# A retention block and two MLPs on one core: another bank for two products at the head, a conversion started one unit later, and a new order of a seven-product pair

## The chip, the cores and the metric

The program runs on one core of one Trainium2 chip. A core has five engines that run side by side and wait for each other through semaphores: PE (TensorE, matrix products), DVE (VectorE), ACT (ScalarE), POOL (GpSimd) and SP (SyncE, which here only issues transfers). Every engine works through its own list of instructions in order. Results of PE go to banks of PSUM, a small memory of eight banks; ACT and DVE read them from there. The metric is the time of one execution on the device in microseconds (us), the median of several runs.

## The reference, cut to what matters

```python
# retention: 2 batches, 8 heads, 768 positions, 64 wide, blocks of 64
intra = (qb @ kb.T * Dmask) @ vb
inter = (qb * lam_pow) @ kv_state
out[block] = intra + inter
kv_state = lam_block * kv_state + (kb * rev_pow).T @ vb
...
x = out as 1536 tokens x 512
h = max(x @ w_in, 0);  x = (h * h) @ w_out        # first MLP, 2048 hidden
h = x @ w_in2;         y = max(0.01 * h, h) @ w_out2   # second MLP
```

The four weight matrices are float64, everything else is float32.

## The kernel before

**Retention** (function `retention`) takes the two batches in 12 units of 128 positions. For each unit, PE transposes k and q (`transposes`, L287 to L300; PE rows with L294), ACT copies the two banks to `kT` and `qT` (L298), PE makes the products of q and k (`scores`, L311), DVE multiplies them with the decay table `DTr` (`mask`, `Pm`, L316), DVE scales q for the carried state (`scale_q`, `qS`, L304), PE makes the new state's product (`state`, L335; it takes `kd`, a decayed k of POOL) and the output (`output`, L360 and L362). ACT and DVE then split the output into a high and a low part, `xhi` and `xlo` (`split`, L68 and L69). The order of PE and SP is that of the code (a manual schedule); the order of ACT, DVE and POOL is set by the scheduler. `bank()` hands out the next PSUM bank in turn, and the instruction that writes it first has to wait until the bank's last reader is through. A bank named `idle` takes transposes without use at the very start.

**Conversion of weights.** A megabyte of float64 words (a tile `raw`) is loaded by SP, and `converting` turns it to float32 step by step: an absolute value on ACT (L114, tile `hb`), six steps on DVE (L115, L116, L118, L121, L122, L125), then a cast of the high part on ACT (L135) and the low part on DVE (L137). `convert()` takes one step at each call. In retention it is called once a unit, for the units 3 to 9, with the step pinned to its place in the order.

**MLPs.** A layer takes the hidden 2048 in four slices s, and the 1536 tokens in three tiles of 512. A float32 product is made of three reduced ones: high by high, high by low, low by high (`three`, L503). `first` makes the hidden values of a tile, one bank m of 128 at a time, in 12 products; ACT and DVE make high and low parts of the activation from it: tiles `g0h`, `g0l` of token tile 0 and `g1h`, `g1l` of token tile 1 (index m, 0 to 3). `second` multiplies by the second weights.

For layer 0, slices 1 and 2 (`seven`), the second products of token tiles 0 and 1 are made with seven block products in place of eight (`second_pair`). The blocks of the weights are A11, A12, A22 and the sums S1 to S4; those of the tokens are B11, B21, B22 and the sums T1 to T4 (`four_sums`, DVE L449 to L451; its results are split by a cast on ACT, L68, and a subtraction on DVE, L69). Each of them is done for p = 0 and p = 1, six matrix products each, on a bank per p. Two block products can share a bank: S4 by B22 goes on adding to the bank C of S1 by T1, after this has been copied. `keep` copies a bank with ACT (L609) to a buffer f, and sends it to a tensor in memory: by SP where it is the first value, by POOL with an addition in memory where it is not (L613). The tensors `partial` hold P1 (A11 by B11), P6 and P67; after the last slice of `seven`, ten additions from memory to memory, issued by POOL (L684), combine them.

Of the kernel before, what the change touches and what calls it, by code (L numbers as in the profile page):

```python
# [19 lines left out]
def tile_retention_then_two_mlps(  # L20
# [163 lines left out]
    def retention(ctx_att, att):  # L184
# [9 lines left out]
        nats, qT, kT, qS, Pm, raw_scores = {}, {}, {}, {}, {}, {}  # L194
# [82 lines left out]
        def column_of_powers():  # L277
            ps = bank()[:, 0:H]
            nc.tensor.transpose(ps, pw[:, 1:C + 1], ident[0:H, 0:H])
            nc.scalar.copy(kdec, ps)  # L280
# [7 lines left out]
        def transposes(i, names="kq"):  # L288
            for name in names:
                dst = {"k": kT, "q": qT}[name]  # L290
                ps = bank().rearrange("p (a s) -> p a s", a=NP)
# [31 lines left out]
        def state(n):  # L323
# [8 lines left out]
            ps = bank()[:, 0:NP * D].rearrange("p (a e) -> p a e", a=NP)  # L332
# [51 lines left out]
        state(0)  # L384
        mask(0)
        output(0)
        scale_q(2, transposes(2))
# [3 lines left out]
        for i in range(n_units):  # L391
# [16 lines left out]
            if 3 <= i <= 9:  # L408
                convert(pin=True)
# [195 lines left out]
    partial = [{n: dram.tile([P, TT], F32, name=f"partial{p}{n}") for n in ("P1", "P6", "P67")} for p in range(2)]  # L605
# [11 lines left out]
    def second_pair(s):  # L617
        begun = (0, s - 1) in seven
# [35 lines left out]
        for p in both:  # L654
            keep(product(p, "A", "A11", "B11"), partial[p]["P1"], not begun)
            yield True
        for p in both:
            keep(product(p, "C", "S1", "T1"), kept(p, 1, 1), False)
            yield True
        late_split("T3", "T1", lambda h: (1, 2 * h))  # L660
        for p in both:
            keep(product(p, "A", "A12", "B21", False), kept(p, 0, 0), False)
            yield True
        late_split("T4", "B21", lambda h: (0, 2 * h + 1))
        for p in both:
            keep(product(p, "C", "S4", "B22", False), kept(p, 0, 1), False)
            yield True
        for p in both:
            keep(product(p, "B", "S2", "T2"), partial[p]["P6"], not begun)
            yield True  # L670
# [4 lines left out]
        for p in both:  # L675
            keep(product(p, "B", "S3", "T3", False), partial[p]["P67"], not begun)
            yield True
        opened.add(("sums", 0, s + 1))
        if (0, s + 1) not in seven:
            for p in both:  # L680
                p1, p6, p67 = (partial[p][n] for n in ("P1", "P6", "P67"))
                for dst, src in ((p67, p1), (kept(p, 0, 1), p1), (kept(p, 0, 1), p6), (kept(p, 1, 0), p67),
                                 (kept(p, 1, 1), p67)):
                    nc.gpsimd.dma_start(dst, src, accum_op=ALU.add, max_dma_last_dim=TT)  # L684
# [46 lines left out]
    def stage(l, s):  # L731
# [4 lines left out]
        if l == 0:  # L736
            parts = [first(l, s, t, ms) for ms in (range(2), range(2, 4)) for t in range(2)]
        else:
# [43 lines left out]
```

## Time and profile before

| | |
|---|---|
| runs | 576.01, 576.70 and 577.94 us, median 576.7 |
| profiled execution | 576.42 us, its span 574.5 us |
| PE busy | 564.2 us of the span, 98% |
| DVE, ACT, POOL busy | 418.4, 305.0 and 83.9 us |
| granted TensorE clock | 1.000 over the span |

The span goes from the first instruction to the last; 1.92 us of the profiled execution lie outside of it. Busy time is the time in which an engine had an instruction at work, and the rest is waiting. Products of PE follow each other before the one ahead has ended: a product of 512 columns is listed with 0.39 us, and the next begins after 0.23.

### The profile page before, as it was taken

Reading aid. Unit: us, or ns where it says so; the run is one execution under the profiler, and the core shown is the slowest. Engines: PE = TensorE matmul, PEld = TensorE weight load, DVE = VectorE, ACT = ScalarE, POOL = GpSimd, SP = SyncE. Lnnn points to the kernel's source line nnn. Section 1 sums busy time; section 2 is a strip of 40 time slices with the busy share of each in tenths; the row PEclk is TensorE's granted clock in tenths of the full one; section 3 lists DMA queues with packets and bytes.
Section 4 is the critical chain, followed back from the end, with each engine's and each line's share of the span. In section 5 each row is a group of like instructions: output and inputs, shape, how many; then the busy total and the mean of one; then the engine's idle time right before and its main releaser. Section 6 shows DMA issues by size and latency. Waiting matters only on the chain.

```text
span 574.5 us, 8051 instructions
## 1 busy us (share of the span) xinstructions
PE 564.2 (98%) x3075; PEld 470.7 (82%) x3075; DVE 418.4 (73%) x589; ACT 305.0 (53%) x477; POOL 83.9 (15%) x101
## 2 busy tenths in 40 slices
PE   7989999999999999999999999999999999999997
PEld 6878888888788888888888888888888888888886
DVE  3879999999927599498478999929873996217222
ACT  2344598546757687758448374553562376225110
POOL 3426000000040105445000000000203011310000
PEclk9999999999999999999999999999999999999999
DMA  8997434665492649999713216341529523661432
GB/s 172 239 213 177 156 121 138 234 183 180 172 164 57 73 148 181 203 249 189 185 36 91 76 41 216 128 165 74 103 55 246 109 29 47 76 90 56 162 113 92
DMA packets 74071, 78.12 MB, mean 136 GB/s; under 512 B 40105, under 2 KB 46513, under 8 KB 74033
## 3 DMA queue, kind: packets, MB, share of 16 engines
q1 hardware_dynamic: 60448, 60.57, 34.6%
q0 software_dynamic: 13056, 16.78, 20.9%
q8 instruction: 24, 0.39, 0.3%
q10 hardware_dynamic: 528, 0.26, 0.2%
q14 instruction: 15, 0.11, 0.1%
HBM read 52.43 MB, written 27.80 MB: 140 GB/s over the span
## 4 chain that ended last, share of the span: by engine, by line
PE 74%; DVE 15%; DMA 6%; issue 3%; SPq 1%; ACT 1%; POOL 0%; DVEq 0%; POOLq 0%; ACTq 0%
PE ps L503 72%; DMA raw<-in_moe_w_in 2%; DVE rb L122 2%; DMA raw<-in_moe_w_out 2%; DVE hb L125 2%; DVE hb L118 2%; SPq L65 1%; DVE rb L121 1%; DVE hb L115 1%; DVE Pm L316 1%; DMA k<-in_k 1%; DVE xlo L69 1%; DVE w1l L137 0%; DVE g1l L474 0%; DVE sw L442 0%
## 5 line engine op out<-in xcount | busy, mean ns | idle before, releaser
L503 PE MATMUL ps<-xhi,w1h 128*128 128x512 f32 x288 | 112.1, 389 | 0.0
L503 PE MATMUL ps<-xlo,w1h 128*128 128x512 f32 x288 | 112.0, 389 | 0.0
L503 PE MATMUL ps<-xhi,w1l 128*128 128x512 f32 x288 | 112.0, 389 | 0.0
L613 POOL DMA_DIRECT2D spill<-f x48 | 46.9, 1047 | 347.6 <-ACT f L609 347.5
L609 ACT COPY f<-ps 128x512 f32<-128x512 f32 x84 | 48.9, 586 | 74.1 <-PE ps L503 72.7
L503 PEld LDWEIGHTS ps<-xhi,w1h 128*128 128x128 f32 x288 | 54.1, 188 | 11.3 <-issue 0.2
L503 PEld LDWEIGHTS ps<-xlo,w1h 128*128 128x128 f32 x288 | 54.1, 188 | 11.3
L503 PEld LDWEIGHTS ps<-xhi,w1l 128*128 128x128 f32 x288 | 54.1, 188 | 11.2
L474 DVE TENSOR_TENSOR g0l<-f,g0h 128x512 fp32r<-128x512 f32 x52 | 35.1, 687 | 33.7 <-ACT f L470 22.1
L503 PE MATMUL ps<-w2l,g0h 128*128 128x512 f32 (+1 forms) x132 | 50.5, 383 | 0.0
L503 PE MATMUL ps<-w2h,g0l 128*128 128x512 f32 (+1 forms) x132 | 50.5, 383 | 0.0
L503 PE MATMUL ps<-w2h,g0h 128*128 128x512 f32 (+1 forms) x132 | 50.5, 383 | 0.0
L137 DVE TENSOR_TENSOR w2l<-hb,w2h 128x1024 fp32r<-128x1024 f32 x16 | 19.5, 1222 | 39.8 <-ACT w2h L135 39.8
L114 ACT ACTIVATE hb<-raw 128x1024 f32<-128x1024 f32 x32 | 36.8, 1150 | 19.2 <-DVE w2l L137 7.4
L503 PE MATMUL ps<-g0h,w2h 128*128 128x512 f32 x104 | 40.5, 389 | 0.0
L503 PE MATMUL ps<-g0l,w2h 128*128 128x512 f32 x104 | 40.5, 389 | 0.0
L503 PE MATMUL ps<-g0h,w2l 128*128 128x512 f32 x104 | 40.5, 389 | 0.0
L122 DVE SCALAR_TENSOR_TENSOR rb<-raw,rb 128x1024 f32<-128x1024 uint32 x32 | 39.1, 1221 | 0.4
L125 DVE TENSOR_TENSOR hb<-hb,rb 128x1024 f32<-128x1024 f32 x32 | 39.1, 1220 | 0.4
L118 DVE SCALAR_TENSOR_TENSOR hb<-raw,hb 128x1024 uint32<-128x1024 uint32 x32 | 39.1, 1220 | 0.3
L567 DVE TENSOR_TENSOR f<-ps,f 128x512 f32<-128x512 f32 x40 | 26.2, 684 | 9.9 <-PE ps L503 9.9
L714 DVE TENSOR_TENSOR f<-ps,f 128x512 f32<-128x512 f32 (+1 forms) x25 | 16.7, 669 | 22.9 <-PE ps L503 21.7
(141 smaller groups left out, 1139.4 us busy)
## 6 DMA issues: line engine op xcount, KB each, us to landing
raw<-in_moe_w_in SPq DMA_DIRECT2D x16, 1024.0 KB, 5.6
raw<-in_moe_w_out SPq DMA_DIRECT2D x16, 1024.0 KB, 5.0
spill<-f POOLq DMA_DIRECT2D x48, 256.0 KB, 4.8
spill<-f SPq DMA_DIRECT2D x24, 256.0 KB, 2.6
f<-spill SPq DMA_DIRECT2D x24, 256.0 KB, 2.9
k<-in_k SPq DMA_DIRECT2D x12, 256.0 KB, 4.9
q<-in_q SPq DMA_DIRECT2D x12, 256.0 KB, 5.1
v<-in_v SPq DMA_DIRECT2D x12, 256.0 KB, 4.8
```

The lines of the kernel that those rows point to most:

```text
L65: return nc.sync.dma_start(dst, src)
L114: nc.scalar.activation(hf, w_hi.bitcast(F32), AF.Abs)
L118: yield ve.scalar_tensor_tensor(out=hb, in0=w_hi, scalar=0xC0000000, in1=hb, op0=ALU.bitwise_and, op1=ALU.bitwise_or)
L122: yield ve.scalar_tensor_tensor(out=rf, in0=w_lo, scalar=2.0 ** -52, in1=rf, op0=ALU.mult, op1=ALU.mult)
L125: yield ve.tensor_tensor(out=hf, in0=hf, in1=rf, op=ALU.add)
L137: yield ve.tensor_tensor(out=lo, in0=hf, in1=hi, op=ALU.subtract)
L474: nc.vector.tensor_tensor(out=glo, in0=r, in1=ghi, op=ALU.subtract)
L503: nc.tensor.matmul(ps, a, b, start=start and n == 0, stop=stop and n == len(ops) - 1, skip_group_check=again)
L567: ve.tensor_tensor(out=out, in0=ps[h, where], in1=other, op=ALU.add)
L609: nc.scalar.copy(f, src)
L613: nc.gpsimd.dma_start(dst, f, accum_op=ALU.add)
L714: nc.vector.tensor_tensor(out=a, in0=ps, in1=a, op=ALU.add)
```

## The change

Three things change. At the head of retention, the small transpose of `column_of_powers` writes to the bank `idle`, the transposes of unit 2's k take the bank of unit 1's q, the product of `state(0)` takes the bank of unit 1's k, and the transposes of unit 2's k are written ahead of `mask(0)` and `output(0)`. The pinned steps of conversion are made in the units 4 to 10. In `second_pair`, A11 by B11 comes ahead of the first layer's last bank (m = 3 of token tile 1, which moves into the pair), A12 by B21 comes ahead of S1 by T1, and S4 by B22 follows S1 by T1 directly; each slice has `partial` tensors of its own, and makes its own ten additions.

```diff
         def column_of_powers():
-            ps = bank()[:, 0:H]
+            ps = idle[:, P:P + H]
...
-                ps = bank().rearrange("p (a s) -> p a s", a=NP)
+                whole = bank() if (i, name) != (2, "k") else read[1, "q"]
+                read[i, name] = whole
+                ps = whole.rearrange("p (a s) -> p a s", a=NP)
...
-            ps = bank()[:, 0:NP * D].rearrange("p (a e) -> p a e", a=NP)
+            whole = bank() if n else read[1, "k"]
+            ps = whole[:, 0:NP * D].rearrange("p (a e) -> p a e", a=NP)
...
         state(0)
+        transposes(2, "k")
         mask(0)
         output(0)
-        scale_q(2, transposes(2))
+        scale_q(2, transposes(2, "q"))
         state(1)
...
-            if 3 <= i <= 9:
+            if 4 <= i <= 10:
                 convert(pin=True)
...
-    partial = [{n: dram.tile([P, TT], F32, name=f"partial{p}{n}") for n in ("P1", "P6", "P67")} for p in range(2)]
+    partials = {
+        s: [{n: dram.tile([P, TT], F32, name=f"partial{s}{p}{n}") for n in ("P1", "P6", "P67")} for p in range(2)]
+        for _, s in seven
+    }
...
         for p in both:
-            keep(product(p, "A", "A11", "B11"), partial[p]["P1"], not begun)
-            yield True
+            keep(product(p, "A", "A11", "B11"), partial[p]["P1"], True)
+            yield True
+        yield from first(0, s, 1, (3,))
+        for p in both:
+            keep(product(p, "A", "A12", "B21", False), kept(p, 0, 0), False)
+            yield True
+        late_split("T4", "B21", lambda h: (0, 2 * h + 1))
         for p in both:
             keep(product(p, "C", "S1", "T1"), kept(p, 1, 1), False)
             yield True
         late_split("T3", "T1", lambda h: (1, 2 * h))
         for p in both:
-            keep(product(p, "A", "A12", "B21", False), kept(p, 0, 0), False)
-            yield True
-        late_split("T4", "B21", lambda h: (0, 2 * h + 1))
+            keep(product(p, "C", "S4", "B22", False), kept(p, 0, 1), False)
+            yield True
         for p in both:
-            keep(product(p, "C", "S4", "B22", False), kept(p, 0, 1), False)
-            yield True
-        for p in both:
-            keep(product(p, "B", "S2", "T2"), partial[p]["P6"], not begun)
+            keep(product(p, "B", "S2", "T2"), partial[p]["P6"], True)
             yield True
...
-        if (0, s + 1) not in seven:
-            for p in both:
-                p1, p6, p67 = (partial[p][n] for n in ("P1", "P6", "P67"))
+        for p in both:
+            p1, p6, p67 = (partial[p][n] for n in ("P1", "P6", "P67"))
...
+            if (l, s) in seven:
+                parts[-1] = first(l, s, 1, (2,))
```

On PE at the head, this stands in the order of before, from `scores(1)` (L311) on; L335 is `state(0)`, then L362 `output(0)`, then the transposes (L294) of unit 2:

```order
L311 MATMUL ps<-qT,kT 128x128 x7
L335 MATMUL ps<-v,kd 64x64 [waits DMAHW6_49,DVE_49,Pool_49]
L335 MATMUL ps<-v,kd 64x64 x7
L362 MATMUL ps<-Pm,v 64x128 [waits PE_49]
L362 MATMUL ps<-Pm,v 64x128 [waits DVE_49]
L362 MATMUL ps<-Pm,v 64x128 x6
L294 MATMUL ps<-ident,k 128x128 [waits DMAHW0_49]
```

and this in that of the change, where the same instructions are L313, L338, L365 and L296:

```order
L338 MATMUL ps<-v,kd 64x64 [waits DMAHW6_49,Pool_49]
L338 MATMUL ps<-v,kd 64x64 x7
L296 MATMUL ps<-ident,k 128x128 [waits DMAHW0_49,DVE_49]
L296 MATMUL ps<-ident,k 128x128 x3
L365 MATMUL ps<-Pm,v 64x128 [waits PE_49]
L365 MATMUL ps<-Pm,v 64x128 x7
```

`state(0)` has lost its wait for DVE, and unit 2's k transposes have moved ahead of `output(0)` and gained one (for `scale_q(1)`, the last reader of their new bank).

On ACT, the piece around the first absolute value of the conversion (L114) reads in the change as follows; xhi_282 are the casts of the outputs 0 to 2, kT and qT those of the units 2 to 4:

```order
L300 COPY kT<-ps 128x512
L68 CAST xhi_282<-ps 128x4x128
L300 COPY qT<-ps 128x512
L300 COPY kT<-ps 128x512
L300 COPY qT<-ps 128x512
L68 CAST xhi_282<-ps 128x4x128
L300 COPY kT<-ps 128x512
L300 COPY qT<-ps 128x512
L68 CAST xhi_282<-ps 128x4x128
L114 ACTIVATE hb<-raw 128x1024
```

Before, the first two rows stood the other way round, and the others in the same places; L114 is the eighteenth instruction of ACT in both, and the copies for unit 5 stand behind it in both.

On ACT in the pair of slice 1, before (with the numbers of the tiles: ps_1771 and ps_1782 are the banks C of p = 0 and p = 1, ps_1749 the bank of A11 and A12 for p = 0; casts to g1h are those of T3, casts to g0h those of T4, the cast to t4 that of T2):

```order
L609 COPY f_1778<-ps_1771 128x512 [waits PE_49]
L68 CAST t4_1648<-f_1738 128x512 [waits DVE_49]
L68 CAST g1h_1598<-f_1617 128x512 [waits PE_49]
L68 CAST g1h_1598<-f_1711 128x512 [waits PE_49]
L609 COPY f_1789<-ps_1782 128x512
L609 COPY f_1805<-ps_1749 128x512 [waits DMAHW2_49,PE_49,Activation_49]
```

and in the change, where C is ps_1800 and ps_1814, and A11 and A12 lie on ps_1724 and ps_1738:

```order
L616 COPY f_1780<-ps_1724 128x512 [waits PE_49]
L68 CAST g0h_1554<-f_1592 128x512 [waits PE_49]
L616 COPY f_1790<-ps_1738 128x512 [waits DMAHW1_49,PE_49]
L616 COPY f_1807<-ps_1800 128x512 [waits DMAHW2_49,PE_49]
L68 CAST t4_1651<-f_1763 128x512 [waits DVE_49]
L68 CAST g0h_1554<-f_1692 128x512 [waits DVE_49]
L68 CAST g1h_1601<-f_1620 128x512 [waits PE_49]
L68 CAST g1h_1601<-f_1714 128x512 [waits PE_49]
L616 COPY f_1821<-ps_1814 128x512 [waits Activation_49]
```

Between the copies of the two banks C stand four casts in the change, and three before. In slice 2 the change has three casts between them (two of T3, one of T2).

## Rows read from the trace of the kernel before

**Rows 1.** The page: the span, busy time by engine, and the chain that ended last.

```profile
span 574.5 us, 8051 instructions
PE 564.2 (98%) x3075; PEld 470.7 (82%) x3075; DVE 418.4 (73%) x589; ACT 305.0 (53%) x477; POOL 83.9 (15%) x101
...
PE 74%; DVE 15%; DMA 6%; issue 3%; SPq 1%; ACT 1%; POOL 0%; DVEq 0%; POOLq 0%; ACTq 0%
```

**Rows 2.** Waits of PE: us in total, times, longest us.

```profile
PE ps L335 <- issue: 2.5, 1, 2.5
PE ps L311 <- ACT qT L298: 2.2, 3, 1.8
```

**Rows 3.** Timeline of PE at the head: start, us, instruction [idle before, releaser].

```profile
14.06 0.69 PE L335 MATMUL ps<-v,kd 128*64 128x64 f32 x16 [2.52 <-issue]
...
32.73 1.16 PE L311 MATMUL ps<-qT,kT 64*128 64x128 f32 x16 [1.76 <-ACT qT L298]
```

**Rows 4.** Timeline of DVE in retention, same columns.

```profile
13.27 1.29 DVE L316 TENSOR_TENSOR Pm<-ps,DTr 128x512 f32<-128x512 f32 x2 [6.79 <-DMA DTr<-tab]
...
31.75 1.37 DVE L115 TENSOR_SCALAR hb<-hb 128x1024 f32<-128x1024 f32 x1 [2.71 <-ACT hb L114]
...
56.71 1.22 DVE L137 TENSOR_TENSOR w1l<-hb,w1h 128x1024 fp32r<-128x1024 f32 x1
```

**Rows 5.** Timeline of ACT at the head, around the first absolute value.

```profile
30.60 1.12 ACT L114 ACTIVATE hb<-raw 128x1024 f32<-128x1024 f32 x1 [3.47 <-DMA raw<-in_moe_w_in]
...
32.09 0.59 ACT L298 COPY qT<-ps 128x512 f32<-128x512 f32 x1
```

**Rows 6.** Timeline of SP's queue: the issue of the first weights.

```profile
22.76 1.13 SPq L65 DMA_DIRECT2D raw<-in_moe_w_in  x1
```

**Rows 7.** Windows: us, busy us of each engine (x), clock, DMA share, GB/s.

```profile
64.00:155.00 91.00, 90.91 (x401) 74.95 (x400) 88.74 (x113) 64.06 (x95) 0.00 (x0) 1.00 0.48 160
...
157.00:200.00 43.00, 43.00 (x191) 35.60 (x190) 22.28 (x29) 28.46 (x45) 10.57 (x12) 1.00 0.61 103
200.00:228.00 28.00, 28.00 (x125) 23.19 (x124) 27.90 (x39) 21.91 (x37) 7.40 (x8) 1.00 0.63 156
228.00:280.00 52.00, 52.00 (x231) 43.06 (x230) 35.24 (x45) 35.78 (x54) 20.54 (x21) 1.00 1.08 201
```

**Rows 8.** Timeline of PE in the pair of slice 1: firsts of block products, and the wait.

```profile
151.12 0.39 PE L503 MATMUL ps<-g0h,w2h 128*128 128x512 f32 x1
...
153.84 0.39 PE L503 MATMUL ps<-g1h,sw 128*128 128x512 f32 x1
...
155.44 0.50 PE L503 MATMUL ps<-g1l,sw 128*128 128x512 f32 x1 [0.53 <-DVE g1l L69]
...
157.40 0.39 PE L503 MATMUL ps<-g0h,w2h 128*128 128x512 f32 x1
...
160.12 0.39 PE L503 MATMUL ps<-g1h,sw 128*128 128x512 f32 x1
```

**Rows 9.** Timeline of ACT in the pair of slice 1.

```profile
157.59 0.62 ACT L68 CAST t<-f 128x512 fp32r<-128x512 f32 x1 [0.79 <-DVE f L450]
158.12 1.14 ACT L68 CAST g1h<-f 128x512 fp32r<-128x512 f32 x2
159.16 1.06 ACT L609 COPY f<-ps 128x512 f32<-128x512 f32 x2
```

**Rows 10.** Timeline of DVE before and in the pair of slice 1.

```profile
147.35 0.69 DVE L450 TENSOR_TENSOR f<-f 128x512 f32<-128x512 f32 x1
...
154.70 0.69 DVE L69 TENSOR_TENSOR g1l<-f,g1h 128x512 fp32r<-128x512 f32 x1
```

**Rows 11.** Timeline of ACT in the pair of slice 2: the copy of bank C.

```profile
218.80 0.59 ACT L609 COPY f<-ps 128x512 f32<-128x512 f32 x1 [0.61 <-PE ps L503]
```

**Rows 12.** Timeline of DVE in the pair of slice 2.

```profile
216.54 1.22 DVE L125 TENSOR_TENSOR hb<-hb,rb 128x1024 f32<-128x1024 f32 x1
```

**Rows 13.** Waits of POOL: the longest ahead of an addition in memory.

```profile
POOL spill L684 <- DMA spill<-f: 5.8, 1, 5.8
```

## What the change does to the time: the prediction

> **What bounds the kernel now.** The page comes first: PE is busy 98% of the span, and three quarters of the chain that ended last are PE's own [rows 1]. The granted clock is 1.00 in the windows from 64 to 280 us [rows 7], so a product costs the same there. What can be won without removing products is PE's idle time, 574.5 − 564.2 = 10.3 us. The list of PE's waits names the ones that this change is about: 2.5 us ahead of `state(0)` and 1.8 us ahead of one of the `scores` [rows 2]. The timeline puts them at 14.06 and 32.73 us [rows 3], and a third of 0.53 at 155.44, in the pair of slice 1 [rows 8]. The reader is to see next what ends each of them, because a wait that is removed only pays if no later one is anchored to something that has not moved.
>
> **The head.** The wait before 14.06 is put down to "issue", but DVE's first `Pm` starts at 13.27 after 6.79 us of waiting for the decay table [rows 4]; `state(0)` was to write the bank that this `Pm` reads. In the order of the change its wait for DVE is gone. `state(0)` and what hangs on it can then start up to 2.5 us earlier. `output(0)` needs `Pm` and cannot, and the k transposes of unit 2 now wait for `scale_q(1)`, which is behind that `Pm` on DVE.
>
> What is late next is the wait at 32.73. ACT waits 3.47 us for the first weights, makes the absolute value from 30.60 on, and only then copies kT and qT of unit 5, the latter at 32.09 [rows 5]; PE's `scores` start when it is through, 32.09 + 0.59 = 32.68. The weights are issued at 22.76 in SP's row of loads [rows 6]. In the order of the change that issue and the absolute value stand where they did, ahead of the same copies. So whatever PE gains before 32.73 it waits there: 1.76 us become up to 1.76 + 2.52 = 4.28, and **the head is worth 0**. The bounds are 0 and, if the load landed so much earlier, −4.3 (the two waits together).
>
> **The conversion.** The step on DVE that filled part of the stall at 31.75 (L115, 1.37 us) [rows 4] moves behind `Pm` of unit 5, and every later step by one unit. The same steps are made, so their sum is unchanged; but DVE has lost one step's place in a stretch in which it waits, and makes it in one in which it is full: 88.74 of 91 us from 64 to 155 [rows 7]. It enters that stretch later by about that step, 0.7 to 1.4 us. The low part of the first weights was made at 56.71 [rows 4]; a unit takes about 4.5 us (12 units by 64), so it moves to 61.2 and, with the lag, to at most some 63, and the MLP's first products are at 64. This costs PE nothing, with about 1 us of cover left. If that cover were gone, PE would wait for it one for one.
>
> **The pair of slice 1.** Twelve products, one block for both p, take 153.84 − 151.12 = 2.72 us [rows 8]. S1 by T1 took 157.40 − 153.84 = 3.56, so the wait that is listed with 0.53 costs 0.84 from start to start. It ended when DVE had made the low part of T1 (154.70 + 0.69) [rows 10]. In the new order A11 runs from 148.40, m = 3 from 151.12, A12 by B21 from 153.84, S1 by T1 from 156.56, S4 by B22 from 159.28. The second half of T1 is now wanted at about 157.5; even with DVE 1.4 us later it is there at 156.8. **This gives −0.84.** A11's low part of bank 2 is wanted at 149.3; DVE makes it straight behind the row at 147.35 [rows 10], so it is ready about 148.7, and 1 us of delay there would show as a short wait.
>
> The new order brings a new wait. S4 by B22 goes on in the bank C of S1 by T1, and must wait for ACT's copy of it. Before, A12 by B21 lay between: from 157.40, when S1 by T1 had ended, to 160.12 [rows 8]. ACT had three casts to make first, from 157.59 on, and its copy of p = 1 began at 159.16 [rows 9] and took about 0.57 of the 1.06 for two: done at 159.73, which is 2.33 us after the block's end, inside the 2.72. Now only the six products for p = 0 lie between, 1.36 us. With the same lateness PE waits 2.33 − 1.36 = 0.97. Four casts stand there now in place of three (0.53 more), but the casts may begin at another time: the first hangs on a sum of DVE (L454, which was L450) over the bank m = 3. Step by step: m = 3 ends at 153.84, three activations of ACT end at about 155.9, DVE's three steps of 0.69 or less ahead of that sum and the sum itself (with up to 1 us of lag) end at 158.5 to 159.5, and four casts of 0.53 and the copy end at 161.3 to 162.4, against 160.64 when PE would begin p = 1. That is a wait of 0.7 to 1.8. It cannot be under 0.37: the casts of T3 overwrite what p = 1 reads, so two of them (1.06) and the copy (0.57) come after 159.28 whatever DVE does, with 0.1 for the signals. **I take +1.0**, the measured lateness, bounds 0.4 and 1.9.
>
> The Trainium skill bears on this in "PSUM — Partial Sum Buffer", "Engine vs sequencer instructions": the queues of ScalarE and VectorE are strictly first in, first out. By that rule the copy cannot overtake casts that wait for DVE, and the sum would be that of this paragraph; ACT's rows in the pair [rows 9] agree, the copy following the casts though its bank was full 1.76 us before.
>
> **The pair of slice 2.** The copy of C for p = 0 began at 218.80, when PE had filled it [rows 11]. In the new order the same block comes 2.72 later, so p = 1 ends at 218.75 + 1.36 + 2.72 = 222.8 and S4 by B22 wants its bank at 224.2. DVE, at 216.54 in L125 [rows 12], has eight instructions ahead of the end of L454; by the rows' durations (two of 1.22, seven of 0.69, starts a little closer) that ends at 223.1 to 223.8. Then the T2 cast and the copy, 1.1 together: 224.2 to 225.0. The least is 0.37 as above. **+0.5**, bounds 0.4 and 1.0.
>
> **Transfers.** Ten additions in memory are made once more, and six sums of slice 2 become plain stores. POOL's queue then works from about 165 to 200, where PE has no idle time and the DMA share is 0.61 [rows 7]; before, this work fell into the stretch from 228 on, at 1.08, where PE lost nothing either. By counts of 2.72 S3 by T3 ends at 181 (two blocks after 162.0, four banks of token tile 2, one block); two dependent additions with a wait of up to 5.8 us each [rows 13] and the stores of token tile 2 then leave POOL by about 200, and land by about 206. The buffers f that these free are wanted for m = 2 and the pair of slice 2, from about 212 on. I cost it at 0; if it makes the first weights of the next slice late, DVE, full from 200 to 228 (27.90 of 28) [rows 7], has no slack to give.
>
> The skill's "DMA: Bandwidth & Descriptors", "Issuing engines are not separate DMA queues", speaks against this part: transfers of all issuers run on the same 16 engines and interleave, so POOL's additions would take their share from SP's loads. No row of before shows the two together at that place. What it would do is the fourth rival below.
>
> **Sum.** 576.42 − 0.84 + 1.0 + 0.5 + 0 = 577.1 us on the profiled execution, which lies 0.3 below the median of 576.7. By the bounds: 576.42 − 0.84 + 0.8 = 576.4 to 576.42 − 0.84 + 2.9 + 0.5 (a wait at A11) = 579.0. I predict 577.2. A difference of 0.3% (1.7 us, 575.0 to 578.4) is about what a measurement of this kernel can tell from no change.
>
> **The rivals.**
> - *The head pays* (chance 0.22). The first weights land earlier since less stands ahead of them, or ACT's copies are not held; then 2.5 to 4.3 us go, and the waits of the pairs come on top: 577.1 − 2.5 = 574.6, at the best 572.8. For it speaks that the wait of 2.5 is surely released; against it that the 32.73 start hangs on the landing alone [rows 3, 5, 6].
> - *The copy is in time* (0.15): DVE is early and the waits are at their least, 576.4, or none, 575.6. The data dependence of T3's casts speaks against none.
> - *DVE is late* (0.17): its lag of 1.4 meets a full stretch [rows 7], and PE also waits at 64 us or at A11 and for T2, by 1 to 2 us: 578.5 to 579.5, slower. It decides when the lag passes the 1 us of cover.
> - *Additions hold up loads* (0.06): the combination from 165 to 200 delays the weights of slice 2 or the buffers f by more than the 6 us they have, each us beyond lost: 579 to 582.
> - The forecast itself has 0.40, its own range 576.4 to 579.0.
>
> **How the numbers follow.** Leaving out the best of the first rival and the fourth gives 574.2 to 579.6. Faster by over 0.3%: the most of the first rival and a bit of the second, 0.22. Slower: the third and fourth, and the forecast's upper end, 0.25. Within: 0.53.
>
> **What would show it.** In the changed profile the wait before `state(0)` is gone, and the one before `scores` near 32.7 is over 3 us, ended by ACT's qT; no wait for `g1l` in the first pair, but one for ACT's copy in each pair, about 1.0 and 0.5 us. Wrong would be a start of those `scores` before 31.5, a first-pair wait over 2 us or none, or a wait of PE between 33 and 148 us.

## The result, and the profile after

The changed kernel takes 583.51 us (median of 5 runs, 583.02 to 584.7), the kernel before beside it 576.43 (575.83 to 577.94): a ratio of 1.0123 (95% interval 1.0108 to 1.0138), so slower by 7.1 us. The profiled execution of the changed kernel took 584.70 us, 1.2 above its median. The forecast was 577.2 in a range from 574.2 to 579.6; it was wrong, on the slow side.

The page of the changed kernel, its span, busy time and the chain that ended last (against [rows 1]):

```profile
span 582.8 us, 8049 instructions
PE 567.8 (97%) x3075; PEld 472.3 (81%) x3075; DVE 418.7 (72%) x589; ACT 304.6 (52%) x477; POOL 87.7 (15%) x105
...
PE 70%; DVE 15%; DMA 7%; ACT 4%; issue 3%; SPq 1%; DVEq 0%; ACTq 0%
```

The span grew by 8.3 us. PE's idle time went from 10.3 to 15.0 (+4.7), and its busy time by 3.6 although it makes the same 3075 products; at least in part these ran at a lower clock. PE's waits, against [rows 2]:

```profile
PE ps L507 <- ACT f L616: 3.7, 2, 2.4
PE ps L296 <- DVE qS L306: 2.2, 1, 2.2
PE ps L313 <- ACT qT L300: 1.7, 2, 1.5
PE ps L507 <- DVE g0l L492: 1.6, 1, 1.6
```

The timeline of PE in the changed kernel says where, against [rows 3, 8] (start, us, instruction, idle before and releaser):

```profile
12.03 0.69 PE L338 MATMUL ps<-v,kd 128*64 128x64 f32 x16
14.87 0.66 PE L296 MATMUL ps<-ident,k 128*128 128x128 f32 x4 [2.15 <-DVE qS L306]
...
32.76 1.16 PE L313 MATMUL ps<-qT,kT 64*128 64x128 f32 x16 [1.47 <-ACT qT L300]
...
65.06 0.50 PE L507 MATMUL ps<-xhi,w1h 128*128 128x512 f32 x1
...
149.53 0.39 PE L507 MATMUL ps<-g0h,w2h 128*128 128x512 f32 x1
...
152.18 0.50 PE L507 MATMUL ps<-g0l,w2h 128*128 128x512 f32 x1 [1.58 <-DVE g0l L492]
...
166.23 0.50 PE L507 MATMUL ps<-g1h,sw 128*128 128x512 f32 x1 [2.38 <-ACT f L616]
168.33 3.89 PE L507 MATMUL ps<-t,sw 128*128 128x512 f32 x12
172.06 0.40 PE L507 MATMUL ps<-g0h,w2h 128*128 128x512 f32 x1
...
174.79 0.39 PE L507 MATMUL ps<-xhi,w1h 128*128 128x512 f32 x1
...
232.05 0.50 PE L507 MATMUL ps<-g1h,sw 128*128 128x512 f32 x1 [1.34 <-ACT f L616]
```

The reader is to see three things. At the head nothing came of the change: `state(0)` lost its wait, the transposes behind it have one of 2.15, and the scores that started at 32.73 before start at 32.76. Up to 148 us there is little: PE waits 0.46 us for DVE's carried state (`st`) at 62.71, and the layer's first product starts at 65.06 where it started at 63.95. Then come two waits in the pair of slice 1, at A11's low part and at bank C. The first product behind the pair (token tile 2, m = 0) sums them up. It starts at 174.79 above, and here before:

```profile
168.28 0.39 PE L503 MATMUL ps<-xhi,w1h 128*128 128x512 f32 x1
```

The lag of PE is 65.06 − 63.95 = 1.1 us at the entry, 149.53 − 148.40 = 1.1 where m = 2 ends, and 174.79 − 168.28 = 6.5 behind the pair, which costs 5.4. The waits make 1.58 + 2.38; the 0.84 of T1's low part is saved. The rest is mostly the clock: from the end of the second wait at 166.23 to the next block's start at 172.06 lie 18 products, which take 5.83 us where 18 × 0.227 are 4.08, 1.75 us more. The windows of the changed kernel, against [rows 7], show the granted clock with it (us, busy us of PE, PEld, DVE, ACT and POOL with counts, clock, DMA share, GB/s):

```profile
100.00:130.00 30.00, 30.00 (x134) 24.85 (x133) 25.57 (x32) 14.64 (x20) 0.00 (x0) 1.00 0.54 185
157.00:200.00 43.00, 40.62 (x173) 33.09 (x172) 22.10 (x32) 26.36 (x42) 17.81 (x20) 0.96 0.92 155
165.00:170.00 5.00, 3.77 (x10) 2.98 (x11) 1.58 (x3) 2.25 (x5) 2.29 (x3) 0.70 0.83 119
228.00:280.00 52.00, 50.66 (x223) 41.61 (x223) 40.02 (x52) 35.12 (x54) 20.89 (x21) 1.00 1.12 221
```

A mean of 0.70 over the 5 us behind the wait is a stretch at the lower of the clock's two levels (1.2 of 2.4 GHz) and one at the full level. Slice 2 adds its wait of 1.34. So 1.1 at the entry, 5.4 in the pair of slice 1 and 1.3 in that of slice 2 are 7.8 of the 8.3 us.

Why both waits: ACT's rows in the pair (against [rows 9]) show the casts held by DVE's sum, and the copies of bank C behind them:

```profile
163.31 0.62 ACT L68 CAST t<-f 128x512 fp32r<-128x512 f32 x1 [1.55 <-DVE f L454]
164.03 0.62 ACT L68 CAST g0h<-f 128x512 fp32r<-128x512 f32 x1
164.56 1.13 ACT L68 CAST g1h<-f 128x512 fp32r<-128x512 f32 x2
165.60 1.06 ACT L616 COPY f<-ps 128x512 f32<-128x512 f32 x2
```

DVE made that sum (L454) from 162.59 to 163.28; the forecast had it end by 159.5. DVE was already late long before the pair. In the window from 100 to 130 it was busy for 25.57 us, before the change for 28.64:

```profile
100.00:130.00 30.00, 30.00 (x134) 24.86 (x133) 28.64 (x34) 15.58 (x21) 0.00 (x0) 1.00 0.63 208
```

These are SP's, ACT's and DVE's rows around one of those gaps, in the changed kernel:

```profile
108.20 0.38 SPq L65 DMA_DIRECT2D raw<-in_moe_w_out  x1
112.46 0.38 SPq L65 DMA_DIRECT2D raw<-in_moe_w_out  x1
...
119.66 1.13 ACT L114 ACTIVATE hb<-raw 128x1024 f32<-128x1024 f32 x1 [3.39 <-DMA raw<-in_moe_w_out]
...
120.82 0.70 DVE L115 TENSOR_SCALAR hb<-hb 128x1024 f32<-128x1024 f32 x1 [1.60 <-ACT hb L114]
```

and these of before, for the same two loads:

```profile
104.16 0.38 SPq L65 DMA_DIRECT2D raw<-in_moe_w_out  x1
110.11 0.38 SPq L65 DMA_DIRECT2D raw<-in_moe_w_out  x1
...
115.02 1.16 ACT L114 ACTIVATE hb<-raw 128x1024 f32<-128x1024 f32 x1 [1.19 <-DMA raw<-in_moe_w_out]
```

A load is issued when DVE has read the buffer that it overwrites (in the changed kernel the last reader, L122, runs from 106.95 to 108.17, and the load follows at 108.20). Before, the two are issued 5.95 us apart and ACT starts 4.91 us after the second issue; after the change they are 4.26 apart and ACT starts 7.20 us after it, and DVE waits for ACT. The Trainium skill says in "DMA: Bandwidth & Descriptors", "Issuing engines are not separate DMA queues", that transfers run on the same 16 engines and interleave. ACT begins with the first of the two at 113.60, 1.14 us after the second is issued, so they can have shared the engines for that long at most; no run here shows what made the second one late, and `f3_extra` below has the same spacing without a late load.

The load is one gap of several. DVE is idle for 4.43 of these 30 us: 1.60 in the gap above, 0.33 in another for a load, and twice 1.12 while ACT casts the sums of the weights (`sw`, L445), where `e4_head_pair` below, which has before's conversion steps, has one such gap (1.11):

```profile
104.00 1.23 DVE L446 TENSOR_TENSOR sw<-rb,sw 128x1024 fp32r<-128x1024 f32 x1 [1.12 <-ACT sw L445]
...
128.11 1.23 DVE L446 TENSOR_TENSOR sw<-rb,sw 128x1024 fp32r<-128x1024 f32 x1 [1.12 <-ACT sw L445]
```

In the pair itself DVE's order differs too. Each sum is made twice; the rows show the first L455 and the second L454, the one on which the casts above wait. In `e4_head_pair` they are

```profile
144.14 1.22 DVE L118 SCALAR_TENSOR_TENSOR hb<-raw,hb 128x1024 uint32<-128x1024 uint32 x1
...
146.49 0.69 DVE L121 TENSOR_SCALAR rb<-hb 128x1024 uint32<-128x1024 uint32 x1
...
148.29 0.68 DVE L455 TENSOR_TENSOR f<-f 128x512 f32<-128x512 f32 x1
...
157.63 0.68 DVE L454 TENSOR_TENSOR f<-f 128x512 f32<-128x512 f32 x1
```

and these in the changed kernel:

```profile
152.05 0.68 DVE L455 TENSOR_TENSOR f<-f 128x512 f32<-128x512 f32 x1
152.65 1.22 DVE L118 SCALAR_TENSOR_TENSOR hb<-raw,hb 128x1024 uint32<-128x1024 uint32 x1
...
155.59 0.69 DVE L121 TENSOR_SCALAR rb<-hb 128x1024 uint32<-128x1024 uint32 x1
...
162.59 0.69 DVE L454 TENSOR_TENSOR f<-f 128x512 f32<-128x512 f32 x1
```

Two steps of conversion, L118 and L121, stand behind that L455 where they stood ahead of it. So L455 is 3.76 us late, and L454, on which the casts wait, 4.96: 1.20 of it comes behind L455.

### The profile page after: what moved, and what is told of

It is laid out like the page before. It is cut to its first block, busy times and chain, and to the rows that moved or that the text cites. A ratio compares the mean times of both kernels' runs of the same rounds, so it can differ in the third digit from the quotient of the medians.

```text
span 582.8 us, 8049 instructions
## 1 busy us (share of the span) xinstructions
PE 567.8 (97%) x3075; PEld 472.3 (81%) x3075; DVE 418.7 (72%) x589; ACT 304.6 (52%) x477; POOL 87.7 (15%) x105
## 4 chain that ended last, share of the span: by engine, by line
PE 70%; DVE 15%; DMA 7%; ACT 4%; issue 3%; SPq 1%; DVEq 0%; ACTq 0%
PE ps L507 68%; DMA raw<-in_moe_w_in 4%; DVE rb L122 2%; DVE hb L125 2%; DVE hb L118 1%; SPq L65 1%; DMA raw<-in_moe_w_out 1%; ACT hb L114 1%; DVE rb L121 1%; DMA q<-in_q 1%; DVE Pm L318 1%; DVE hb L115 1%; PE ps L363 1%; DVE w2l L137 1%; DVE hb L116 1%
## 5 line engine op out<-in xcount | busy, mean ns | idle before, releaser
L114 ACT ACTIVATE hb<-raw 128x1024 f32<-128x1024 f32 x32 | 36.7, 1148 | 20.9 <-DMA raw<-in_moe_w_in 6.5
L122 DVE SCALAR_TENSOR_TENSOR rb<-raw,rb 128x1024 f32<-128x1024 uint32 x32 | 39.7, 1239 | 0.4
L118 DVE SCALAR_TENSOR_TENSOR hb<-raw,hb 128x1024 uint32<-128x1024 uint32 x32 | 39.1, 1221 | 0.4
```

The costliest lines, as they stand in the source:

```text
L114: nc.scalar.activation(hf, w_hi.bitcast(F32), AF.Abs)
L118: yield ve.scalar_tensor_tensor(out=hb, in0=w_hi, scalar=0xC0000000, in1=hb, op0=ALU.bitwise_and, op1=ALU.bitwise_or)
L122: yield ve.scalar_tensor_tensor(out=rf, in0=w_lo, scalar=2.0 ** -52, in1=rf, op0=ALU.mult, op1=ALU.mult)
```

## The experiments

Three theories were held against each other at first: the parts add up (P), one part alone makes the loss (H), or a DVE that enters late meets the shortened distance to bank C's copy (S).

**The parts alone.** `e1_head` is the kernel before with the head's lines of the change, `e3_pair` with those of the pair and the partials, `e2_conv` with this line:

```diff
-            if 3 <= i <= 9:
+            if 4 <= i <= 10:
                 convert(pin=True)
```

and `e4_head_pair` is the changed kernel with this line set back.

> The kernel before with the head's edits alone (banks, and unit 2's k transposes ahead of output(0)). Theory S (the shifted conversion makes DVE late and the pair pays for it): the head is worth nothing, 576.1 to 577.0 us, with the scores of unit 5 still starting at 32.7. Theory P (the new order in the pair costs by itself): the same. Theory H (the head's new wait for scale_q costs): above 577.5.

> The kernel before with the conversion's steps in the units 4 to 10 alone. Theory S: DVE is about 2 us late at 64 us and about 4 us at 150 us, and the old order of the pair waits longer for the low part of T1: 3 to 5 us slower, 579.5 to 581.5 us. Theory P: the conversion is hidden, 576 to 577.5 us.

> The kernel before with the new order of the pair and the partial tensors of each slice alone. Theory S: DVE is early enough, so the wait for A11's low part is gone, the one for the copy of bank C is about 0.7 to 1 us in slice 1 and up to 1.3 in slice 2, against 0.84 won: 576.5 to 578.5 us. Theory P: the waits are as in the changed kernel, 4 to 6 us slower, 580.5 to 582.5 us.

> The changed kernel with the conversion back in the units 3 to 9. Theory S: as the new order of the pair alone, 576.5 to 578.5 us. Theory P: 580 to 583 us.

Measured, ratio to before with interval: head 576.46 us, 0.9993 (0.9980 to 1.0006); conversion 579.09 (just under theory S's 579.5 to 581.5), 1.0045 (1.0024 to 1.0065); pair 577.97, 1.0028 (1.0013 to 1.0042); head and pair 578.24, 1.0030 (1.0016 to 1.0044). So the head is worth 0, the pair loses 1.6 us, and the conversion 2.6 with before's own pair, where PE waits twice (PE's timeline of `e2_conv`):

```profile
156.54 0.50 PE L503 MATMUL ps<-g1h,sw 128*128 128x512 f32 x1 [1.32 <-ACT g1h L68]
158.35 0.79 PE L503 MATMUL ps<-g1l,sw 128*128 128x512 f32 x1 [1.31 <-DVE g1l L69]
```

Together the parts would make 4.2 to 4.3; the change costs 7.1. H falls, and P leaves some 2.8 us, give or take about 1.7 (an estimate from the intervals).

**Is it the stall at the head, or unit 10?** `e5_two_steps` takes the step out of the stall in the kernel before, but ends in unit 9; `f1_after_two` is the same edit in the changed kernel.

```diff
-            if 3 <= i <= 9:
-                convert(pin=True)
+            if 4 <= i <= 9:
+                for _ in range(2 if i == 4 else 1):
+                    convert(pin=True)
```

> The kernel before with the conversion's steps in the units 4 to 9, two of them in unit 4: the first step leaves the stall at 31.75, but the last one stands where it stood before. Theory E (DVE's last step at the entry of the MLP, its 1.2 us in a full stretch, starts the lag): about the time of before, 576 to 577 us. Theory F (the step that no longer fills the stall is the cost): as the shift alone, 578.5 to 580 us.

> The changed kernel with its pinned conversion steps in the units 4 to 9, two of them in unit 4, so that all seven are made by unit 9. Theory E (what costs is only that the seventh step is made in unit 10, where DVE has no gap left, so that it enters the MLP about 1.2 us later and the late loads make 4 us of it): 578.0 to 578.7 us, ratio about 1.003, PE's waits for ACT's copy of bank C 2 to 2.5 us together, none at A11's low part. Rival (what costs is that the first weights are begun a unit later at all, together with the new pair): 582 to 584 us, ratio 1.010 or more, with the wait for g0l at A11.

Measured: 576.64, 1.0002 (0.9993 to 1.0012), and 578.1, 1.0028 (1.0013 to 1.0044). Taking the step out of the stall costs nothing; that the last one falls into unit 10 costs all of the conversion's part, and its interaction too.

**The pair's distance.** `e6_s2_first` (on `e4_head_pair`) and `e7_after_s2` (on the changed kernel) put S2 by T2 between S1 by T1 and S4 by B22; `e8_shared` gives `e4_head_pair` before's shared partial tensors; `f2_split` takes A12 by B21 apart in `e4_head_pair`, and `f5_after_split` in the changed kernel:

```diff
-        for p in both:
-            keep(product(p, "A", "A12", "B21", False), kept(p, 0, 0), False)
-            yield True
-        late_split("T4", "B21", lambda h: (0, 2 * h + 1))
+        keep(product(0, "A", "A12", "B21", False), kept(0, 0, 0), False)
+        yield True
         for p in both:
             keep(product(p, "C", "S1", "T1"), kept(p, 1, 1), False)
             yield True
         late_split("T3", "T1", lambda h: (1, 2 * h))
+        keep(product(1, "A", "A12", "B21", False), kept(1, 0, 0), False)
+        yield True
+        late_split("T4", "B21", lambda h: (0, 2 * h + 1))
```

> Head and pair without the shift, and S2 by T2 set between S1 by T1 and S4 by B22. Theory C (PE waits for the copy of bank C since only one half block lies between): the copy is hidden in slice 1, 0.7 us less; in slice 2 PE waits for T2's low part in its place, so about the same there: 577.0 to 578.0 us. Theory D (DVE's sums are late in the pair whatever the order): no change, 578.2 us.

> The changed kernel with S2 by T2 set between S1 by T1 and S4 by B22. Theory C: the wait of 2.4 us for the copy goes in part, and the lowered clock behind it goes or is shorter: 1 to 3 us less than the changed kernel, 580.5 to 582.5 us. Theory D: DVE is late for T2 by as much, and the time is the changed kernel's, 583 to 584 us.

> Head and pair without the shift, with the partial tensors shared by both slices as before, so that no additions in memory run between them. Theory L (slice 1's additions make the weights of 200 us land 1.7 us late, DVE 1.25 us, and so the T2 cast and the copy in slice 2): slice 2's wait falls from 1.6 to about 0.4 us, 576.8 to 577.3 us. Rival: the additions are hidden and the wait is that of the order, 578.0 to 578.5 us.

> Before's conversion steps with the new head and the new pair, in which A12 by B21 is taken apart: p = 0 ahead of S1 by T1, p = 1 behind it and ahead of S4 by B22. Twelve products (2.72 us) then lie between the end of S1 by T1 for p = 1 and the second use of its bank, as before, and S1 by T1 is still wanted 1.36 later. Theory C (the pair's loss is the short distance to the copy of bank C alone): the waits for that copy fall from 2.3 us to at most 0.4, 575.8 to 576.6 us, ratio 0.998 to 1.000. Rival D (ACT and DVE are late in the pair anyway, and PE waits for the next thing of theirs, T1's low part or T2): 577.5 to 578.5 us, ratio 1.002 to 1.003, the waits under another name.

> The changed kernel, conversion in the units 4 to 10, with A12 by B21 taken apart as before: p = 0 ahead of S1 by T1, p = 1 behind it. Theory M (the two parts multiply: the late DVE costs much only because the new pair leaves 1.36 us to the copy of bank C): DVE is as late in slice 1 as in the changed kernel (L454 around 162 to 163 us), the wait at A11's low part stays at 1 to 2 us, the wait at bank C of slice 1 falls from 2.4 us to about 1, the granted clock between 165 and 170 us stays at 1.00 where it was 0.70, 578.5 to 580.5 us, ratio 1.004 to 1.007. Rival A (the parts only add, the distance is worth the same 2.1 us as without the late steps): 581 to 582 us, ratio about 1.009, a wait over 2 us in slice 1 and a clock under 1.00 again.

Measured: `e6_s2_first` 579.37, 1.0059 (1.0037 to 1.0081), `e7_after_s2` 582.38, 1.0101 (1.0078 to 1.0124). The waits for bank C went and waits for T2 came (1.4 for ACT's cast and 0.7 for DVE's low part, in slice 2, in `e6_s2_first`): the block that was to cover the copy needs what DVE makes last. `e6_s2_first` came out above both of its theories. `e8_shared` 578.42, 1.0043 (1.0023 to 1.0062): the partials of each slice's own cost nothing that the time can show, but the traces differ. From 195 to 200 us, and on ACT, `e4_head_pair` has

```profile
195.00:200.00 5.00, 5.00 (x24) 4.14 (x23) 4.86 (x7) 3.47 (x6) 1.52 (x2) 1.00 1.25 154
...
207.15 1.12 ACT L114 ACTIVATE hb<-raw 128x1024 f32<-128x1024 f32 x1 [1.74 <-DMA raw<-in_moe_w_in]
```

and `e8_shared`

```profile
195.00:200.00 5.00, 5.00 (x23) 4.14 (x23) 4.78 (x6) 3.24 (x7) 0.00 (x0) 1.00 0.43 52
...
205.62 1.14 ACT L114 ACTIVATE hb<-raw 128x1024 f32<-128x1024 f32 x1
...
223.88 0.59 ACT L613 COPY f<-ps 128x512 f32<-128x512 f32 x1 [2.79 <-DMA partial1P<-f]
```

The load for this L114 is issued at 200.02 and 200.33. With slice 1's additions in memory just ahead of it (DMA share 1.25 against 0.43), ACT begins 7.13 us after the issue in place of 5.29, and DVE's L454 of slice 2 starts at 223.94 in place of 222.91. What `e8_shared` wins by that it loses again: a copy waits 2.79 us for a buffer whose value POOL adds to the shared P1, and PE waits 1.44 and 0.38 us for copies in slice 2 in place of 1.62. So theory L had the cause of DVE's lateness there, and not the time.

`f2_split` 576.1, 0.9988 (0.9974 to 1.0001): the waits for bank C, in the waits of PE of `e4_head_pair` and of `f2_split`,

```profile
PE ps L507 <- ACT f L616: 2.3, 2, 1.6
```

```profile
PE ps L507 <- ACT f L616: 0.3, 1, 0.3
```

went from 2.3 to 0.3 with twelve products between, and so did the pair's loss. This version is 7 us under the changed kernel; that it is under the kernel before is not shown. `f5_after_split` 580.2, 1.0081 (1.0056 to 1.0106), was inconclusive between its two theories: its median lies in the one's range, its ratio nearer the other's. The wait at bank C was 1.7, there was none at A11, and the clock from 165 to 170 us stayed at 1.00; yet the late step still costs 4.1 us by the medians of the two split kernels, and 5.4 by their ratios, as much as with the short distance. So these runs do not show that the short distance is what makes the late step dearer in the new pair than in before's; that stays open.

**Lag or order.** If a late entry is enough, any instruction will do. `f3_extra` adds one to `e4_head_pair`:

```diff
+        spare = att.tile([P, 2, NP, C], F32, name="spare")
...
+            if i == 10:
+                tc.keep_in_program_order(ve.tensor_tensor(out=spare, in0=DTr, in1=DTr, op=ALU.mult))
```

> Before's conversion steps (units 3 to 9) with the new head and the new pair, and one more DVE instruction of 128x1024 pinned in unit 10, a product into a spare tile that nobody reads (about 1.2 us, work added, nothing left out). Theory E (a late entry of DVE by 1.2 us is enough, whatever the instruction is): 580.5 to 583 us, ratio 1.007 or more, DVE's sum L454 of slice 1 about 3 us or more later than in the kernel without the extra instruction, PE waits over 2 us at bank C or A11 in slice 1. Rival (DVE makes up 1.2 us before 150 us, and it is the place of the steps of conversion that costs): 578 to 579 us, ratio 1.003 to 1.004, PE's waits as without the extra instruction.

Measured: 583.31, 1.0124 (1.0098 to 1.0149): 5.1 us for an instruction of 1.23, and the whole loss of the changed kernel. L454 of slice 1 starts at 160.16, in `e4_head_pair` at 157.63; PE waits 2.37 at bank C, and the clock from 165 to 170 us is 0.66. But the instruction does two things. It delays DVE, and it makes the scheduler write another order: apart from the added instruction, the listing of DVE's 516 rows differs from that of `e4_head_pair` in 217 lines (280 for the changed kernel, 13 for `f1_after_two`). `h1_small` cuts the instruction to 128x128 in unit 10, `h3_one_in_8` puts the long one into unit 8, `h2_two_in_7` two of them into unit 7, and `k1_384` makes it 128x384 in unit 10.

> As the kernel with one more DVE instruction in unit 10 (583.3 us), but the instruction is 128x128 in place of 128x1024, some 0.25 us in place of 1.2. It still turns the scheduler's order of DVE from the layer's entry on to nearly that of the kernel with the long one (48 rows of difference to it, 191 to the kernel without). Theory L (the lag does it, growing through late loads): with a fifth of the lag, 578.2 to 579.3 us, ratio 1.003 to 1.005, L454 of slice 1 no more than 0.5 us later than the 157.63 of the kernel without. Theory O (the order does it): 582 to 584 us, ratio 1.010 or more, L454 at about 160 us, PE waits of over 2 us at bank C of slice 1.

> The same long instruction (128x1024, about 1.2 us) pinned in unit 8 in place of unit 10: DVE has no gap from there to the layer, so that it enters it about 1.1 us later, but the scheduler's order is, the extra instruction aside, row for row that of the kernel without it. Theory L: 581.5 to 584 us, ratio 1.009 or more, DVE's L454 of slice 1 at 160 us or later, PE waits of over 2 us at bank C. Theory O: 578.2 to 579.6 us, ratio 1.003 to 1.006, L454 at most 1.2 us later than 157.63, the waits as without the extra instruction, up to 1 us more.

> Two of the long instructions, pinned in unit 7: about 2.3 us of lag, and the old order but for 11 rows. Theory L: 584 us or more, ratio 1.014 or more, as twice the lag meets the full stretch. Theory O: 579 to 581 us, ratio 1.005 to 1.009, the lag showing once, as a wait of PE for DVE in retention or at the layer's entry, and a lag in slice 1 of no more than 2.3.

> The kernel with the new head and the new pair and before's conversion steps, with one more DVE instruction of 128x384 (about 0.45 us from start to start) pinned in unit 10. With 128x256 or less the scheduler keeps the old order of the conversion's raw reads from slice 0 on; with this one it turns them as in the slow kernels (fifth read 0.6 later, sixth 1.1 earlier in DVE's work, ninth 1.1 later). Theory O (the order alone does most of it): DVE waits over 1 us more between 100 and 130 us, L454 of slice 1 at 159.5 us or later, 580.5 to 583 us, ratio 1.007 or more. Theory L (the lag, in whatever order): 578.3 to 579.4 us, ratio 1.003 to 1.0055, L454 at no more than 158.2.

The counts of rows in the first of these were mistaken: `h1_small` differs in 30 lines from the kernel without the instruction and in 219 from the one with the long one, so that it has the old order too and is no test of the other; `k1_384` is (209 lines). Measured, with the two loads' issue (the rows of SP above) and DVE's busy time from 100 to 130 us:

| kernel | DVE's order | loads issued at, apart | DVE busy, of 30 | time, ratio |
|---|---|---|---|---|
| e4_head_pair | old | 104.01, 5.95 | 28.64 | 578.24, 1.0030 |
| f1_after_two | old (13) | 105.53, 5.95 | 28.67 | 578.1, 1.0028 |
| h1_small | old (30) | 104.25, 5.95 | 28.59 | 578.2, 1.0031 |
| h3_one_in_8 | old (0) | 104.70, 5.96 | 28.62 | 579.1, 1.0048 |
| h2_two_in_7 | old (11) | 106.66, 5.95 | 28.62 | 580.49, 1.0067 |
| k1_384 | other (209) | 104.92, 4.26 | 27.53 | 581.0, 1.0089 |
| f3_extra | other (217) | 107.47, 4.25 | 27.22 | 583.31, 1.0124 |
| changed kernel | other (280) | 108.20, 4.26 | 25.57 | 583.51, 1.0123 |

The other kernels fall on the same two sides: `e2_conv`, `e7_after_s2` and `f5_after_split` with 4.26 and 24.86, 25.21 and 27.17, all others with before's conversion steps, or with seven steps by unit 9, and no pinned slice 0, with 5.94 to 5.96 and 28.60 to 28.67. So the gaps of DVE come with the order. They are not the late load's alone: in `f3_extra` and `f5_after_split` ACT begins 5.62 and 5.61 us after the second issue, with the same spacing, and DVE does not wait for that load. The waits of `f3_extra` in this window are both for the cast of `sw` (its lines are shifted by three; the text keeps the numbers of the changed kernel):

```profile
103.27 1.23 DVE L449 TENSOR_TENSOR sw<-rb,sw 128x1024 fp32r<-128x1024 f32 x1 [1.12 <-ACT sw L448]
...
125.90 1.23 DVE L449 TENSOR_TENSOR sw<-rb,sw 128x1024 fp32r<-128x1024 f32 x1 [1.18 <-ACT sw L448]
```

So a late load is not needed for the loss. What `f3_extra` shares with the changed kernel is the place of L118 and L121 behind L455: its L455 is 1.32 us late (149.61) and its L454 2.53. In `k1_384`, where L118 stands ahead, they are 0.60 and 0.62 late.

A lag of 2.6 us with the old order (`h2_two_in_7`, whose first L115 behind the added instructions starts at 64.46, in `e4_head_pair` at 61.85) opens none, and costs once what it weighs: 2.3 us by the medians for two instructions of 1.23. A lag of 0.45 us with the other order (`k1_384`) opens them and costs 2.8.

What this doesn't settle: in `h3_one_in_8` and `h2_two_in_7` PE waits for DVE in retention and shares the lag (its first layer product starts at 64.52 and 66.38), so that DVE is hardly late against PE. And in `k1_384` L454 was only 0.62 us late; PE's further wait there came by another way, a copy of ACT that had no buffer because the store of P1 was late (ACT's timeline of `k1_384`):

```profile
159.20 0.59 ACT L621 COPY f<-ps 128x512 f32<-128x512 f32 x1 [1.91 <-DMA partial10P<-f]
```

So `k1_384` has theory O's time without its late L454 (159.5 or later was expected). That the order costs beyond the lag is shown by its time and by DVE's gaps; how the 5 us of `f3_extra` and of the changed kernel divide between lag and order is not.

**The order held the same.** `j1_pinned` and `j3_pinned_extra` are `e4_head_pair` and `f3_extra` with `convert(pin=(l, s) == (0, 0))` in the loop over the stages, so that the scheduler can't move the steps of slice 0.

> The kernel with the new head and the new pair and before's conversion steps (578.24 us), with the steps of conversion in slice 0 of the first layer pinned to their place in the program too, so that the scheduler can't move them. It is the base for the next run; its own time may differ by the pinned order, which releases some weights up to 11 us of DVE work later: 577 to 582 us. If DVE waits over 3 us in the windows from 64 to 150, where it waited 1.4 to 2 without pins, the pair of runs can't tell the theories apart.

> The same with the long DVE instruction (128x1024) pinned in unit 10; the order of all other DVE instructions is the same row for row. Theory L (the lag alone, growing through late loads): 4 to 6 us slower than the run without it, as the 583.3 against 578.2 without pins. Theory O (the scheduler's other order made most of it): 0 to 1.3 us slower, DVE's rows from 100 us on later by at most the 1.2 us of the instruction, and no DVE wait more.

Measured: 582.47, 1.0087 (1.0054 to 1.0121), and 582.05, 1.0085 (1.0056 to 1.0115). The instruction costs nothing here, but by the condition that was set the pair tells nothing: the pinned order leaves DVE 30.02 us of 36 busy from 64 to 100, and those gaps swallow the instruction.

## Why the prediction was wrong, step by step

- **The head: right.** Worth 0, as `e1_head` shows, and for the reason given: the scores follow the landing of the first weights. ACT begins with these at 30.60 and the scores at 32.73 before, at 30.62 and 32.76 after, at 29.80 and 32.00 in `e1_head`. What would show it was put wrongly in size: not a wait of over 3 us there but 1.47, since the transposes' new wait (2.15), which the forecast had named without a price, took the gain first.
- **The conversion: the step that failed.** "This costs PE nothing, with about 1 us of cover left." The lag at the entry had the size that was given (DVE's last `Pm` of retention starts at 61.05, 1.10 us later), and the low part of the first weights came at 63.15 where 61.2 to 63 was said (the 4.5 us a unit are not 64 by 12, which is 5.3). But PE met the lag already there, by the wait of 0.46 for `st`, and began the layer 1.1 us late. And the lag at the entry was all that was priced. "The same steps are made, so their sum is unchanged" held for the amount of DVE's work and not for its order. The runs show in its place that the scheduler wrote another order for all of slice 0, that DVE waited more in it (25.57 of 30 us busy in place of 28.64), that two more of its steps stand ahead of L454 in the pair, and that L454 came 5 us late (162.59 against 157.63 in `e4_head_pair`). How much of this the lag alone would have made stays open. It costs 2.6 us with before's pair and 5.4 with the new one, by the ratios.
- **The low part of A11.** Its delay "would show as a short wait": 1.58, with L454, ahead of it on DVE, at 150.84 where `e4_head_pair` has it at 147.09; 1 us had been allowed for.
- **T1's low part: right.** No wait for g1l is left in the changed kernel or in `e4_head_pair`.
- **Bank C in slice 1: right in mechanism.** With DVE in time the wait is 0.65 (`e4_head_pair` and `e3_pair`), inside 0.4 to 1.9; with DVE late 2.38, outside, because the end of L454 (163.28) lay outside the bounds set for it (158.5 to 159.5). The Trainium skill's rule in "PSUM — Partial Sum Buffer", "Engine vs sequencer instructions", that ScalarE's queue is strictly first in, first out, held to the row: the copies at 165.60 stand behind casts that wait for DVE. And `f2_split` shows the term itself: with the old distance it is 0.3 with DVE in time (and 1.74 with DVE late, in `f5_after_split`).
- **Bank C in slice 2: mis-sized.** Taken as 0.5 (0.4 to 1.0); 1.62 in `e4_head_pair`, 1.34 in the changed kernel, 0.92 in `e3_pair`. The cast and the copy took the 1.1 us that were given, and S4 by B22 wanted its bank at 224.19, as said; the sum L454 ended at 224.63 in `e4_head_pair` where 223.1 to 223.8 was said. Without the additions (`e8_shared`) it ended at 223.59, inside.
- **Transfers: mis-sized at 0.** The forecast named the case, "if it makes the first weights of the next slice late, DVE, full from 200 to 228 (27.90 of 28) [rows 7], has no slack to give", and gave it no price in the sum. It came: 1.8 us on that load and 1.0 on L454 of slice 2, by `e4_head_pair` and `e8_shared`. This is the mechanism of the fourth rival (0.06) at a smaller size, and it is where the term of slice 2 went wrong. That its removal would save time is not shown.
- **The clock** stood in no term. It was priced at 1.00 throughout, and took 1.75 us behind the longest wait.

The rival that came nearest was "DVE is late", at 0.17 and 578.5 to 579.5. It named A11 as a place, but took the lag as fixed and added it once, where it is met at A11, at bank C and in the clock.

## What to carry to other kernels

Where a scheduler sets an engine's order, an instruction moved on it is not one instruction's time: compare the whole listing of that engine's order, to the next place where PE waits for it, and look which of the moved steps now stand ahead of it. Here an instruction of 1.23 us cost 0.9 us in unit 8, where it left the order as it was, and 5.1 in unit 10, where it turned it. Additions in memory that fall just ahead of a load belong in the sum when the engine behind that load is full. And between the first use of a bank and its next one, count what stands ahead of the copy on the copying engine: a block split into halves gave back the distance at no cost (`f2_split`), as long as DVE was in time.

## What the runs showed of the hardware that was not expected

The granted clock fell behind a single long wait of PE, and the slower products behind it cost about three quarters of the wait once more. From 165 to 170 us it was 0.70 and 0.66 behind waits of 2.38 and 2.37 (the changed kernel and `f3_extra`); the 18 products behind the wait took 5.83 and 5.82 us in place of 4.08. In `e2_conv` it was 0.81 and 0.85 from 155 to 165, where two waits of 1.32 and 1.31 stand 1.81 apart. It stayed at 1.00 behind one of 1.74 (`f5_after_split`), and behind 1.36 and 0.91 that stand 2.57 apart (`k1_384`). In the changed kernel the wait of 2.38 cost 2.38 + 1.75. Each of these is one profiled execution.

Additions in memory just ahead of a load made it late: with slice 1's additions in front of it, ACT began 6.0 to 8.2 us after the issue of the load near 200 us, and in the kernels without them 5.3 to 5.5.
